# Pair 0 of an attention kernel: key loads on 64 partitions, early value loads, another order of the first loads, and identity transposes inside the first tile

## The chip, the cores and the metric

The kernel runs on one core of a Trainium2 chip. The metric is device time in microseconds (us) of one execution. Engines are named as in the profile: PE is the matrix engine (PEld its weight loads), DVE the vector engine, ACT the scalar engine, POOL is GpSimd, SP issues the loads and stores.

## What is computed

Attention, then a feed-forward block with an ELU, then a gated block with a norm ahead of it. The change touches only the start of the attention. Cut to that:

```python
B, H, S, D = 2, 8, 1152, 64
q_pool = q.reshape(B, H, S // 2, 2, D).mean(axis=3)      # 576 pooled queries a head
scores = (1 / sqrt(D)) * q_pool @ k.transpose(0, 1, 3, 2)  # 576 x 1152 a head
attn = softmax(scores)
out = attn @ v                                           # then the two blocks
```

## The kernel before

**Heads and tiles.** The 16 heads are taken as 8 pairs. A pair has 9 tiles of 128 query columns against all 1152 keys (TILES, line 30): four of each head and one, number 2 (M = 2), that holds the 64 queries left over of both heads. One loop step (line 531) makes one tile's scores (emit_S: 6 matmuls of 384 keys, 12 for tile 2), transposes the tile of two steps earlier (emit_T: 9 PE transposes, each group of three copied by ACT and DVE), runs 8 matmuls against the values (AV), and takes the exponential (emit_exp, ACT). DVE reads each score tile out of its PSUM bank (line 332); the bank has one buffer, so the scores of the next step wait for that. Pair 0 takes its tiles in the order 0, 1, 3, 4, 2, 5, 6, 7, 8, so head 1 comes first and tile 2, the first to need head 0, is step 4. Later pairs take them as numbered, so tile 2 of pair 1 is step 11.

**Two parts of each number.** Queries, keys and values are split into a rounded part and the rest (hi and lo) by two instructions, on ACT and DVE, or on POOL alone. For keys the product needs the rounded part on partitions 0 to 63 and the rest on 64 to 127. The key array in memory holds each head's 64 rows twice, so one load brings both copies to 128 partitions; hi is made on all 128 and lo then overwrites the upper 64 (prep_k).

**Loads.** All loads are issued by SP in program order, and a load whose buffer is not free holds all that stand behind it. Keys come in two halves of 576 columns (288 KB as loaded), the queries of a head in one load of 576 KB (two numbers to be added for each pooled query, line 292), the values in one of 288 KB. Raw keys and values share two buffers (tag raw), the raw queries have one (rawq); the two key halves of head 0 of pair 0 use the buffers of the later weight loads (rawk0). The queries of head 1 of pair 0 (rawq0) are loaded and prepared in three pieces.

**Order of preparation.** After pair 0's own first parts, each step prepares what jobs lists for it (line 457) and then issues the load of the next part in that list (fetch). Written as kind, pair, head, half, the list begins k 0 0 1 (step 0), v 0 1 (step 2), q 1 1 and v 0 0 (step 3), k 1 1 0 and k 1 1 1 (step 4), v 1 1 (step 5), q 1 0, k 1 0 0, k 1 0 1 (steps 6 to 8). From step 4 on POOL does all of it, in this order. After step 4's parts SP also issues the two first weight loads of 512 KB (ws.load). Ahead of the loop stand 24 identity transposes on PE (line 482), into a PSUM tile that nobody reads.

Of the kernel before, what the change touches and what calls it, by code (L numbers as in the profile page):

```python
# [20 lines left out]
QS = 576  # L21
# [18 lines left out]
def tile_kernel(ctx: ExitStack, tc: tile.TileContext, qd, kd, vd, w1d, w2d, wgd, wvd, wod, rgd, outd):  # L40
    nc = tc.nc
    V, G, T, PE, SP = nc.vector, nc.gpsimd, nc.scalar, nc.tensor, nc.sync
# [4 lines left out]
    ident = const.tile([128, 128], F32, name="ident")  # L47
# [26 lines left out]
    class Stream:  # L74
# [12 lines left out]
        def load(self, n):  # L87
            while self.loaded < min(n, len(self.srcs)):
                i = self.loaded
                t = wp.tile([128, 512, 2], U32, tag="wr", name="wr", bufs=2 if wide else 3)  # L90
                r = t.rearrange("p c w -> p (c w)")
                if wide:
                    SP.dma_start(out=r, in_=self.srcs[i].bitcast(U32))
                else:
                    t = f(r)[:, 0:512]
                    SP.dma_start(out=t, in_=self.srcs[i])
                self.raw[i] = t
                self.loaded += 1
# [171 lines left out]
    def load(kind, p, j, half=0):  # L270
        if kind == "q":
            t = ap.tile([128, 2, QS], F32, tag="rawq", name="rawq", bufs=1)
            SP.dma_start(out=t, in_=qd[2 * p + j].rearrange("p (u c) -> p u c", u=2))
        elif kind == "k":
            if (p, j) == (0, 0):
                t = f(wp.tile([128, 512, 2], U32, tag="wr", name="rawk0", bufs=2 if wide else 3).rearrange("p c w -> p (c w)"))[:, 0:QS]
            else:
                t = ap.tile([128, QS], F32, tag="raw", name="rawk", bufs=2)
            SP.dma_start(out=t, in_=kd[2 * p + j][:, half * QS:(half + 1) * QS])
        else:  # L280
            t = ap.tile([128, 9, 64], F32, tag="raw", name="rawv", bufs=2)
            SP.dma_start(out=t, in_=vd[2 * p + j].rearrange("p (k d) -> p k d", k=9))
        return t

    def prep_q(p, j, t, eng, cols=((0, QS),)):

        hi, lo = eng
        if (p, j) not in QD:
            QD[p, j] = qt[len(QD) % 3]
        d, qp = QD[p, j], t[:, 0, :]  # L290
        for a, b in cols:
            (V if hi is hi_dve else G).tensor_tensor(out=qp[:, a:b], in0=qp[:, a:b], in1=t[:, 1, a:b], op=ALU.add)
            h, l = (d[:, u, 64 + a:64 + b] for u in range(2))
            hi(h, qp[:, a:b])
            lo(l, qp[:, a:b], h)

    def prep_k(p, j, half, t, eng):
        hi, lo = eng
        if half == 0:
            KD[p, j] = ap.tile([128, S], F32R, tag="kd", name="kd", bufs=3)  # L300
        d = KD[p, j][:, half * QS:(half + 1) * QS]
        hi(d, t)
        lo(d[64:128], t[64:128], d[64:128])

    def prep_v(p, j, t, eng):
        hi, lo = eng
# [4 lines left out]
    POOL, DVE = (hi_pool, lo_pool), (hi_dve, lo_dve)  # L311
# [5 lines left out]
    def emit_S(p, i):  # L317
        if i == 0:
            st[p] = ap.tile([128, 4, NPT, 1], F32, tag="st", name="st", bufs=2)
        s = (tp if (p, i) == (0, 1) else sp).tile([128, 3, 512], F32, tag="s", name="s", bufs=1)  # L320
        if i == M:
            parts = [(QD[p, j][:, u, c:c + 128], KD[p, j]) for j, c in ((1, 0), (0, 576)) for u in (0, 1)]
        else:
            j, c, _, _, _ = TILES[i]
            parts = [(QD[p, j][:, u, c:c + 128], KD[p, j]) for u in (0, 1)]
        for n, (a, b) in enumerate(parts):
            for m in range(3):
                PE.matmul(s[:, m, 0:384], lhsT=a, rhs=b[:, 384 * m:384 * m + 384],  # L328
                          start=n == 0, stop=n == len(parts) - 1)
        pt = P[p, i] = ap.tile([128, 3, 384], F32, tag="p", name="p", bufs=3)  # L330

        V.tensor_scalar(out=pt, in0=s[:, :, 0:384], scalar1=-0.0625, scalar2=None,  # L332
                        op0=ALU.mult, op1=ALU.min, accum_out=st[p][:, 0, TILES[i][4], :])
# [106 lines left out]
    ACT = (lambda o, i: T.copy(o, i), lo_dve)  # L440

    def do_prep(u, eng):
        {"q": prep_q, "k": prep_k, "v": prep_v}[u[0]](*u[1:], raws.pop(u), eng)

    raws = {}

    def fetch(u):
        if u not in raws:
            raws[u] = load(*u)
# [7 lines left out]
    jobs = {n: [] for n in range(-1, ns)}  # L457
    for n in range(ns):
        p, k = n // NPT, n % NPT
        if p == 0:  # L460
            u = {0: [("k", 0, 0, 1)], 2: [("v", 0, 1)], 3: [("v", 0, 0)]}.get(k, [])
            jobs[n] += u
        if k in plan and not (p == 0 and k == 1):
            u = plan[k](p)
            if u[1] < 8:
                jobs[n + (p == 0 and k < 4)].append(u)
    order = [u for n in range(ns) for u in jobs[n]]
    t = ap.tile([128, 3, 384], F32, tag="p", name="rawq0", bufs=3).rearrange("p a b -> p (a b)")
    t = t.rearrange("p (u c) -> p u c", u=2)
    q01 = qd[1].rearrange("p (u c) -> p u c", u=2)  # L470
    SP.dma_start(out=t[:, :, 64:320], in_=q01[:, :, 64:320])
    fetch(("k", 0, 1, 0))
    fetch(("k", 0, 1, 1))
    for a, b in ((320, 576), (0, 64)):
        SP.dma_start(out=t[:, :, a:b], in_=q01[:, :, a:b])
    first = [("q", 0, 0), ("k", 0, 0, 0)]
    for u in first + order[:1]:
        fetch(u)

    warm = pp.tile([128, 512], F32, tag="o", name="warm", bufs=2)  # L480
    for n in range(24):
        PE.transpose(warm[:, 0:128], ident, ident)
    prep_q(0, 1, t, DVE, ((64, 320),))
    do_prep(("k", 0, 1, 0), ACT)
    do_prep(("k", 0, 1, 1), ACT)
    prep_q(0, 1, t, POOL, ((320, 576), (0, 64)))
    SP.dma_start(out=rg, in_=rgd)
    for u in first:
        do_prep(u, (ACT[0], lo_pool) if u[0] == "k" else POOL)

    def overwrites(i, g):

# [38 lines left out]
    for step in range(ns):  # L531
        emit_S(*steps[step])
        if step == 1:
            tctx.close()
            tp = actx.enter_context(tc.tile_pool(name="psT", bufs=1, space=PSUM))
            tbank = lambda: tp.tile([128, 512], F32, tag="t", name="t", bufs=3)

        due = [w for w in later if w[0] <= step]
        if step >= LT and not due:
            do_T(step)  # L540
        for w in due:
            later.remove(w)
            w[1]()
        do_AV(8, lambda p: later.append((step + 2, lambda: emit_x(p, emit_scale(p)))))
        if step >= LT and due:
            do_T(step)
        emit_exp(*steps[step])
        if step >= LT:
            if steps[step - LT][1] == NPT - 1:
                emit_r(steps[step - LT][0])  # L550
            after_T(step)
        for u in jobs.get(step, []):
            do_prep(u, (ACT[0], lo_pool) if step < 4 and u[0] != "q" else POOL)
            n = order.index(u)
            if n + 1 < len(order):
                fetch(order[n + 1])
        if step == 4:
            ws.load(2)
        ws.step(0, early_ops.get(steps[step], 0))
# [35 lines left out]
    def bank():  # L595

        nonlocal nbank
        n, nbank = nbank % 7, nbank + 1
        if n == 5 and len(psb) == 1:
            with tc.using_default_side("right"):  # L600
                psb.append(ctx.enter_context(tc.tile_pool(name="psC", bufs=2, space=PSUM)))
                ws.bank = ctx.enter_context(tc.tile_pool(name="psW", bufs=1, space=PSUM))
        return psb[n >= 5].tile([128, 512], F32, tag="b", name="b", bufs=2 if n >= 5 else 5)[:, 0:CH]
# [51 lines left out]
    for hf in range(2):  # L655
# [30 lines left out]
        if hf:  # L686
            T.activation(out=dummy, in_=eps, func=AF.Sqrt)
            for c in range(3):
                for n in range(4):
                    m, q = 2 + n // 2, n % 2  # L690
                    if q == 0:
                        b = bank()
# [86 lines left out]
    def unit(i, c, between=None):  # L779
        b = bank(), bank()  # L780
        for n in range(2):
            product(b[n], ws.get(2 * n + i + wi), xchunk(c), True, True)
            if between and n == 0:
                between()
        return i, c, *b
# [14 lines left out]
    first = [unit(0, 0)]  # L800
# [10 lines left out]
    u = [up.tile([128, 12, CH], F32, name=f"u{c}", tag=f"u{c}") for c in range(2)]  # L811
# [46 lines left out]
    b = Branch(2)  # L858
    run([(b, 1), (b, 8), (b, 9), (b, 2)], 2, 4, 2)
    run([(b, 6), (b, 5)], 2, 5)  # L860
    old, b = b, Branch(3)
    run([(b, 1), (old, 7)], 2, 5)
    for n in range(3, 11):
        if n > 3:
            old, b = b, Branch(n)
# [7 lines left out]
    b = Branch(11)  # L873
# [87 lines left out]
```

## Time and profile before

| | us |
|---|---|
| median of 3 runs | 681.26 |
| lowest and highest | 680.08, 681.34 |
| profiled execution, its own time | 681.72 |
| its span, first to last instruction | 679.9 |

| engine | busy us | share of the span |
|---|---|---|
| PE | 668.2 | 98% |
| DVE | 470.1 | 69% |
| ACT | 461.9 | 68% |
| POOL | 407.3 | 60% |

The span leaves out 1.8 us of the execution's own time. Busy time of PE is modelled from pipelined matmuls, so 98% says that PE seldom stands still, and not that it runs at its peak. The mean granted clock of PE over the span is 0.997 of full speed (2.4 GHz).

### The profile page before, as it was taken

The numbers are of one execution on the slowest core, as the hardware profiler recorded it, in microseconds if no ns is written. First come the engines' busy times: TensorE is split into PE (matmuls) and PEld (weight loads), VectorE is DVE, ScalarE is ACT, GpSimd is POOL, SyncE is SP. The second block draws the span as 40 slices with busy tenths as digits, with TensorE's granted clock in tenths as the row PEclk, the third lists the DMA queues.
The fourth block names the chain that finished last, engine by engine and source line by source line (L and its number), as shares of the span: only waits on it lengthen the run. The fifth ranks groups of instructions, "written<-read, shape, count | busy, mean of one in ns | idle before, by whom it ended". The sixth has DMA issues, their size and how long they took to land.

```text
span 679.9 us, 11376 instructions
## 1 busy us (share of the span) xinstructions
PE 668.2 (98%) x4183; PEld 658.0 (97%) x4183; DVE 470.1 (69%) x803; ACT 461.9 (68%) x921; POOL 407.3 (60%) x366
## 2 busy tenths in 40 slices
PE   7999999999999999999999999999999999999997
PEld 6999999999999999999999999999989999999997
DVE  5989998998999875765345656388777776776300
ACT  5988889898988977994458884455667644655300
POOL 5788898988989324773324443457889865313300
PEclk8999999999999999999999999999999999999999
DMA  5532234233223001224231123010334322204200
GB/s 171 206 104 88 91 126 147 88 106 119 88 88 113 25 1 53 90 90 140 94 123 63 63 94 124 31 63 32 125 98 148 124 66 93 94 1 152 73 36 36
DMA packets 21608, 62.34 MB, mean 92 GB/s; under 512 B 2736, under 2 KB 4784, under 8 KB 21552
## 3 DMA queue, kind: packets, MB, share of 16 engines
q1 hardware_dynamic: 21552, 61.62, 27.1%
q8 instruction: 33, 0.54, 0.3%
q14 instruction: 23, 0.19, 0.1%
HBM read 59.25 MB, written 2.36 MB: 91 GB/s over the span
## 4 chain that ended last, share of the span: by engine, by line
PE 87%; POOL 4%; DVE 3%; ACT 3%; DMA 2%; issue 1%; SPq 0%; POOLq 0%; DVEq 0%; ACTq 0%
PE b L216 15%; PE b L217 15%; PE b L218 15%; PE s L328 11%; PE o L372 10%; PE b L714 10%; PE t L346 10%; DMA rawk<-in_k_dram 1%; DVE x L804 1%; POOL kd L64 1%; POOL vd L64 1%; ACT xh L647 1%; ACT p L337 1%; PE t L407 1%; DMA wr<-in_wg_dram 0%
## 5 line engine op out<-in xcount | busy, mean ns | idle before, releaser
L64 POOL TENSOR_TENSOR wl<-wt,wh 128x512 fp32r<-128x512 f32 x68 | 91.6, 1348 | 96.0 <-ACT wh L183 94.7
L217 PE MATMUL b<-xl,wh 128*128 128x384 f32 x356 | 119.8, 337 | 0.0
L216 PE MATMUL b<-xh,wh 128*128 128x384 f32 x356 | 119.8, 337 | 0.0
L218 PE MATMUL b<-xh,wl 128*128 128x384 f32 x356 | 119.7, 336 | 0.0
L332 DVE TENSOR_SCALAR_CACHE_REDUCE p<-s 128x1152 f32<-128x1152 f32 x72 | 97.4, 1353 | 18.8 <-PE s L328 18.4
L70 DVE TENSOR_TENSOR ptl<-t,pth 128x384 fp32r<-128x384 f32 x216 | 106.6, 548 | 3.5 <-ACT pth L354 2.6
L354 ACT CAST pth<-t 128x384 fp32r<-128x384 f32 x216 | 89.2, 487 | 24.2 <-PE t L346 23.4
L328 PE MATMUL s<-kd,qt 128*128 128x384 f32 x480 | 99.1, 344 | 3.7 <-DVE kd L70 2.0
L337 ACT ACTIVATE p<-p,st 128x1152 f32<-128x1152 f32 x72 | 91.5, 1271 | 1.7 <-DVE p L332 1.4
L328 PEld LDWEIGHTS s<-kd,qt 128*128 128x128 f32 x480 | 83.1, 191 | 5.7 <-DVE kd L70 2.5
L346 PE MATMUL t<-ident,p 128*128 128x128 f32 x648 | 85.4, 275 | 0.4 <-DVE p L332 0.4
L372 PE MATMUL o<-pth,vd 128*128 128x256 f32 (+1 forms) x288 | 84.4, 315 | 0.0
L346 PEld LDWEIGHTS t<-ident,p 128*128 128x128 f32 x648 | 73.9, 141 | 6.7 <-DVE ptl L70 3.8
L372 PE MATMUL o<-ptl,vd 128*128 128x256 f32 (+1 forms) x288 | 78.4, 294 | 0.0
L131 DVE TENSOR_SCALAR wm<-wm 128x512 f32<-128x512 f32 x62 | 43.1, 695 | 40.1 <-ACT wm L122 39.9
L217 PEld LDWEIGHTS b<-xl,wh 128*128 128x128 f32 x356 | 66.9, 188 | 0.5 <-POOL xl L64 0.5
L216 PEld LDWEIGHTS b<-xh,wh 128*128 128x128 f32 x356 | 66.9, 188 | 0.1
L218 PEld LDWEIGHTS b<-xh,wl 128*128 128x128 f32 x356 | 66.9, 188 | 0.0
L120 ACT ACTIVATE we<-wr 128x512 uint32<-128x512 uint32 x68 | 45.4, 667 | 26.6 <-DMA wr<-in_wo_dram 13.8
L64 POOL TENSOR_TENSOR gl<-e,gh 128x384 fp32r<-128x384 f32 x37 | 38.9, 1056 | 41.0 <-ACT gh L237 41.0
L216 PE MATMUL b<-gh,wh 128*128 128x384 f32 x180 | 60.9, 338 | 0.0
L218 PE MATMUL b<-gh,wl 128*128 128x384 f32 x180 | 60.5, 336 | 0.0
(183 smaller groups left out, 1520.6 us busy)
## 6 DMA issues: line engine op xcount, KB each, us to landing
wr<-in_w_dram SPq DMA_DIRECT2D x32, 512.0 KB, 3.2
rawk<-in_k_dram SPq DMA_DIRECT2D x32, 288.0 KB, 3.0
rawq<-in_q_dram SPq DMA_DIRECT2D x15, 576.0 KB, 4.0
wr<-in_wg_dram SPq DMA_DIRECT2D x12, 512.0 KB, 3.2
wr<-in_wv_dram SPq DMA_DIRECT2D x12, 512.0 KB, 3.2
wr<-in_wo_dram SPq DMA_DIRECT2D x12, 512.0 KB, 3.3
rawv<-in_v_dram SPq DMA_DIRECT2D x16, 288.0 KB, 2.8
out_dram<-o SPq DMA_DIRECT2D x12, 192.0 KB, 1.8
```

The lines of the kernel that those rows point to most:

```text
L64: G.tensor_tensor(out=o, in0=i, in1=f(h), op=ALU.subtract)
L70: V.tensor_tensor(out=o, in0=i, in1=f(h), op=ALU.subtract)
L216: PE.matmul(out, lhsT=wh[:, k, :], rhs=ah, start=first and k == 0, stop=False)
L217: PE.matmul(out, lhsT=wh[:, k, :], rhs=al, start=False, stop=False)
L218: PE.matmul(out, lhsT=wl[:, k, :], rhs=ah, start=False, stop=last and k == 3)
L328: PE.matmul(s[:, m, 0:384], lhsT=a, rhs=b[:, 384 * m:384 * m + 384], start=n == 0, stop=n == len(parts) - 1)
L332: V.tensor_scalar(out=pt, in0=s[:, :, 0:384], scalar1=-0.0625, scalar2=None, op0=ALU.mult, op1=ALU.min, accum_out=st[p][:, 0, TILES[i][4], :])
L337: T.activation(out=pt, in_=pt, func=AF.Exp, scale=-1.0, bias=st[p][:, 0, TILES[i][4], :], accum_out=st[p][:, 1, TILES[i][4], :])
L346: PE.transpose(ps[:, k, :], src[:, 128 * b:128 * b + 128], ident)
L354: T.copy(oh, re(ps))
L372: PE.matmul(self.o[:, 0:self.N], lhsT=v[:, b, :], rhs=(pth, ptl)[u][:, g["buf"], b, g["c0"]:320], start=self.n == 0, stop=self.n == 17)
L714: PE.matmul(out, lhsT=a[x][:, k, :], rhs=b[y][:, k, :], start=first and (k, x, y) == (0, 0, 0), stop=last and (k, x, y) == (1, 1, 0), skip ...
```

## The change

Six edits, all in the start of pair 0:

- the key halves of pair 0 are loaded to 64 partitions only (144 KB instead of 288 KB); hi goes to partitions 0 to 63, and lo reads those and writes 64 to 127
- the first key half of head 0 is issued by ACT's queue (T), all others by SP as before
- the first query piece (256 columns) is cut in two of 128; the second is prepared on DVE after both key halves
- head 0's keys are loaded and prepared ahead of its queries, both halves before the loop; its queries are prepared in two pieces, the 64 columns that tile 2 needs first
- both value loads of pair 0 are issued at once at the start; in step 3, v 0 0 is prepared ahead of q 1 1 instead of behind it
- the first tile goes third by third, both halves of the sum each, with 8 identity transposes between the first third and the second

```diff
+            if p == 0:
+                t = t[0:64]
+            (T if (p, j) == (0, 0) else SP).dma_start(out=t, in_=kd[2 * p + j][0:t.shape[0], half * QS:(half + 1) * QS])
...
-        hi(d, t)
-        lo(d[64:128], t[64:128], d[64:128])
+        if p == 0:
+            hi(d[0:64], t)
+            lo(d[64:128], t, d[0:64])
+        else:
+            hi(d, t)
+            lo(d[64:128], t[64:128], d[64:128])
...
+        first = (p, i) == (0, 0)
+        for m, n in [(m, n) for m in range(3) for n in range(2)] if first else [(m, n) for n in range(len(parts)) for m in range(3)]:
+            if first and (m, n) == (1, 0):
+                warming(8)
+            a, b = parts[n]
+            PE.matmul(s[:, m, 0:384], lhsT=a, rhs=b[:, 384 * m:384 * m + 384],
+                      start=n == 0, stop=n == len(parts) - 1)
...
-            u = {0: [("k", 0, 0, 1)], 2: [("v", 0, 1)], 3: [("v", 0, 0)]}.get(k, [])
-            jobs[n] += u
+            u = {2: [("v", 0, 1)], 3: [("v", 0, 0)]}.get(k, [])
+            jobs[n] = u + jobs[n]
...
-    SP.dma_start(out=t[:, :, 64:320], in_=q01[:, :, 64:320])
+    load_q(64, 192)
     fetch(("k", 0, 1, 0))
     fetch(("k", 0, 1, 1))
-    for a, b in ((320, 576), (0, 64)):
-        SP.dma_start(out=t[:, :, a:b], in_=q01[:, :, a:b])
-    first = [("q", 0, 0), ("k", 0, 0, 0)]
-    for u in first + order[:1]:
+    load_q(192, 320)
+    load_q(320, 576)
+    load_q(0, 64)
+    for u in ("k", 0, 0, 0), ("k", 0, 0, 1), ("q", 0, 0), *order[:2]:
         fetch(u)
...
-    prep_q(0, 1, t, DVE, ((64, 320),))
+    warming(24)
+    prep_q(0, 1, t, DVE, ((64, 192),))
     do_prep(("k", 0, 1, 0), ACT)
     do_prep(("k", 0, 1, 1), ACT)
+    prep_q(0, 1, t, DVE, ((192, 320),))
     prep_q(0, 1, t, POOL, ((320, 576), (0, 64)))
     SP.dma_start(out=rg, in_=rgd)
-    for u in first:
-        do_prep(u, (ACT[0], lo_pool) if u[0] == "k" else POOL)
+    for half in range(2):
+        do_prep(("k", 0, 0, half), (ACT[0], lo_pool))
+    prep_q(0, 0, raws.pop(("q", 0, 0)), POOL, ((512, 576), (0, 512)))
```

load_q(a, b) is the SP load of columns a to b that stood there before; warming(n) is n identity transposes into the PSUM tile that the 24 already used.

## Rows read from the trace of the kernel before

**Rows 1.** Waits of PE over the whole run: us in total, times, longest

```profile
PE s L328 <- DVE kd L70: 2.0, 2, 1.7
PE b L714 <- POOL tsl L64: 1.6, 1, 1.6
...
PE s L328 <- POOL kd L64: 0.6, 1, 0.6
```

**Rows 2.** Timeline of PE: start, length (us), work, count [idle before <-releaser]

```profile
1.36 4.44 PE L482 MATMUL warm<-ident 128*128 128x128 f32 x24 [1.36 <-POOL ident masks.py:199]
6.13 0.44 PE L328 MATMUL s<-kd,qt 128*128 128x384 f32 x1 [0.33 <-DVE kd L70]
8.29 4.80 PE L328 MATMUL s<-kd,qt 128*128 128x384 f32 x17 [1.71 <-DVE kd L70]
...
18.16 2.32 PE L328 MATMUL s<-kd,qt 128*128 128x384 f32 x12 [0.82 <-DVE p L332]
...
41.16 1.41 PE L328 MATMUL s<-kd,qt 128*128 128x384 f32 x7
43.13 1.15 PE L328 MATMUL s<-kd,qt 128*128 128x384 f32 x5 [0.56 <-POOL kd L64]
```

**Rows 3.** Stretches: busy us (instructions) of PE, PEld, DVE, ACT, POOL; PE's granted clock; loads

```profile
4.75:5.80 1.05, 1.05 (x10) 0.81 (x8) 0.88 (x2) 0.54 (x1) 0.00 (x0) 1.00 1.02 291
5.80:8.20 2.40, 0.44 (x1) 0.19 (x1) 1.00 (x2) 0.67 (x1) 0.62 (x1) 0.98 0.99 364
8.20:11.50 3.30, 3.21 (x10) 3.21 (x11) 1.24 (x2) 0.67 (x1) 2.96 (x7) 0.50 0.56 210
```

**Rows 4.** Timeline of POOL, the first 43 us

```profile
7.58 1.25 POOL L292 TENSOR_TENSOR rawq<-rawq 128x256 f32<-128x256 f32 x1 [6.27 <-DMA rawq<-in_q_dram]
...
9.40 0.73 POOL L64 TENSOR_TENSOR qt<-rawq,qt 128x256 fp32r<-128x256 f32 x1
10.09 0.32 POOL L292 TENSOR_TENSOR rawq<-rawq 128x64 f32<-128x64 f32 x1
...
11.11 1.43 POOL L292 TENSOR_TENSOR rawq<-rawq 128x576 f32<-128x576 f32 x1
...
14.87 2.80 POOL L64 TENSOR_TENSOR kd<-rawk,kd 64x576 fp32r<-64x576 f32 x2
...
24.37 0.68 POOL L61 TENSOR_SCALAR kd<-rawk 128x576 fp32r<-128x576 f32 x1
...
34.95 1.43 POOL L292 TENSOR_TENSOR rawq<-rawq 128x576 f32<-128x576 f32 x1 [3.22 <-DMA rawq<-in_q_dram]
...
41.66 1.41 POOL L64 TENSOR_TENSOR kd<-rawk,kd 64x576 fp32r<-64x576 f32 x1
```

**Rows 5.** Timelines of ACT (first row) and DVE

```profile
4.62 0.67 ACT L440 CAST kd<-rawk 128x576 fp32r<-128x576 f32 x1 [2.39 <-DMA rawk<-in_k_dram]
...
7.48 0.76 DVE L70 TENSOR_TENSOR kd<-rawk,kd 64x576 fp32r<-64x576 f32 x1 [1.40 <-ACT kd L440]
10.29 1.36 DVE L332 TENSOR_SCALAR_CACHE_REDUCE p<-s 128x1152 f32<-128x1152 f32 x1 [2.06 <-PE s L328]
```

**Rows 6.** Single loads issued at 1.45, 2.07, 2.54, 14.82, 24.43: KB, us from issue to landing

```profile
rawk<-in_k_dram SPq DMA_DIRECT2D x1, 288.0 KB, 3.1
...
rawk<-in_k_dram SPq DMA_DIRECT2D x1, 288.0 KB, 4.7
...
rawq<-in_q_dram SPq DMA_DIRECT2D x1, 256.0 KB, 5.0
...
rawq<-in_q_dram SPq DMA_DIRECT2D x1, 576.0 KB, 3.7
...
rawk<-in_k_dram SPq DMA_DIRECT2D x1, 288.0 KB, 2.7
```

**Rows 7.** Timeline of SP's load issues

```profile
2.54 1.20 SPq L475 DMA_DIRECT2D rawq<-in_q_dram  x2
...
26.60 0.33 SPq L282 DMA_DIRECT2D rawv<-in_v_dram  x1
...
27.92 0.43 SPq L273 DMA_DIRECT2D rawq<-in_q_dram  x1
```

More of the change, by code (lines that the diff above doesn't have):

```diff
@@ L278, in load @@
                 t = ap.tile([128, QS], F32, tag="raw", name="rawk", bufs=2)
-            SP.dma_start(out=t, in_=kd[2 * p + j][:, half * QS:(half + 1) * QS])
+            if p == 0:
+                t = t[0:64]
+            (T if (p, j) == (0, 0) else SP).dma_start(out=t, in_=kd[2 * p + j][0:t.shape[0], half * QS:(half + 1) * QS])
         else:
@@ L325, in emit_S @@
             parts = [(QD[p, j][:, u, c:c + 128], KD[p, j]) for u in (0, 1)]
[L326 to L329, printed above, removed]
+        first = (p, i) == (0, 0)
[5 more added lines that the diff above has]
+                      start=n == 0, stop=n == len(parts) - 1)
         pt = P[p, i] = ap.tile([128, 3, 384], F32, tag="p", name="p", bufs=3)
@@ L470, in tile_kernel, with load_q, warming @@
     q01 = qd[1].rearrange("p (u c) -> p u c", u=2)
-    SP.dma_start(out=t[:, :, 64:320], in_=q01[:, :, 64:320])
+    def load_q(a, b):
+        SP.dma_start(out=t[:, :, a:b], in_=q01[:, :, a:b])
+    load_q(64, 192)
     fetch(("k", 0, 1, 0))
     fetch(("k", 0, 1, 1))
-    for a, b in ((320, 576), (0, 64)):
-        SP.dma_start(out=t[:, :, a:b], in_=q01[:, :, a:b])
-    first = [("q", 0, 0), ("k", 0, 0, 0)]
-    for u in first + order[:1]:
+    load_q(192, 320)
+    load_q(320, 576)
+    load_q(0, 64)
+    for u in ("k", 0, 0, 0), ("k", 0, 0, 1), ("q", 0, 0), *order[:2]:
         fetch(u)
     warm = pp.tile([128, 512], F32, tag="o", name="warm", bufs=2)
-    for n in range(24):
-        PE.transpose(warm[:, 0:128], ident, ident)
-    prep_q(0, 1, t, DVE, ((64, 320),))
+    def warming(n):
+        for _ in range(n):
+            PE.transpose(warm[:, 0:128], ident, ident)
+    warming(24)
+    prep_q(0, 1, t, DVE, ((64, 192),))
     do_prep(("k", 0, 1, 0), ACT)
     do_prep(("k", 0, 1, 1), ACT)
+    prep_q(0, 1, t, DVE, ((192, 320),))
     prep_q(0, 1, t, POOL, ((320, 576), (0, 64)))
     SP.dma_start(out=rg, in_=rgd)
-    for u in first:
-        do_prep(u, (ACT[0], lo_pool) if u[0] == "k" else POOL)
+    for half in range(2):
+        do_prep(("k", 0, 0, half), (ACT[0], lo_pool))
+    prep_q(0, 0, raws.pop(("q", 0, 0)), POOL, ((512, 576), (0, 512)))
     def overwrites(i, g):
```

## The prediction

> **What bounds the kernel now.** I read the waits of PE first. The change is confined to pair 0, and PE waits for little anywhere: 2.0 us in the first tile for the keys that DVE finishes, 0.6 us for keys that POOL finishes, and much later 1.6 us in another stage [rows 1]. So PE sets the time wherever it doesn't wait, and the question is what those early waits are worth. The timeline of PE places them. The 24 identity transposes end at 5.80; one matmul of the first tile runs at 6.13; then PE stands until 8.29 for the second key half. The 0.56 us for POOL stand at 43.13, inside step 11: tile 2 of pair 1 has run its seven first matmuls and waits for the last key half of head 0 of that pair [rows 2].
>
> That second wait is the important one. The timeline of POOL shows why it is there. POOL prepares everything for pair 1 in one long queue, and the last piece ends at 41.66 + 1.41 = 43.07, which releases PE at 43.13 [rows 2, 4]. Back from there POOL works without a pause to 34.95, where it had waited 3.22 us for the raw queries of pair 1's head 0 [rows 4]. That load was issued at 27.92, behind a value load issued at 26.60 and two weight loads of 512 KB [rows 7]. The value load waited for the buffer of the first key half of pair 1, which POOL began at 24.37 and so let go about 2.2 us later [rows 4, 7]. So step 11 goes on at a time that POOL's queue and SP's queue set, not PE: a fixed 16.5 us after the key half is prepared (43.07 - 26.57). **Whatever PE gains before step 11, it waits out there, unless that key half is prepared earlier too.**
>
> **The first tile.** Removed: half of the bytes of four key loads, 128 of the query columns ahead of them, and the wait for the second half with one matmul done. The first key half keeps its place in SP's queue (1.45, landing 3.1 us later [rows 6]). The second landed 4.7 us after its issue at 2.07, with 832 KB of loads up to and with it; now these are 416 KB. A single load of 288 KB took 2.7 us [rows 6], so it lands between 4.75 and 6.75; I take 5.0, near the lower end, since the bytes ahead halve. ACT's copy (0.67) and DVE's rest (0.76 [rows 5]) go by columns, not partitions, so I keep both: keys ready at about 6.45. PE is held by its transposes to 5.80, runs two matmuls at 0.18 each (12 took 2.32 us with the tail of the last [rows 2]), and 8 transposes at 0.105 (ten in 1.05 us [rows 3]) or at 0.185 (24 in 4.44 us [rows 2]): to 7.0 or 7.6. Four more matmuls end at 7.7 to 8.4. DVE reads the tile from about 7.9 instead of 10.29 [rows 5]: 2.4 us earlier. The added transposes cost 0.8 to 1.5 us of PE, of which 0.3 to 0.9 lie beside the wait for the keys. Had they cost all of it, it would still vanish in step 11.
>
> The second tile then runs at once and at full clock, where before its scores ran at half clock in part (0.50 from 8.2 to 11.5 [rows 3]); that gives 0.3 us more. Step 4, at 18.16 before [rows 2], needs head 0's keys; POOL had them at 14.87 + 2.80 = 17.67 [rows 4] and now has them near 13 (below), so POOL holds nothing there. I take PE to be 2.6 us ahead from step 4 on, between 2.0 and 3.0. It reaches step 11 at 38.6 instead of 41.16.
>
> **POOL's queue, where the end is set.** Its first work is the third query piece. That load is now fourth behind the first instead of third: two pieces were issued in 1.20 us from 2.54 [rows 7], so it moves from 2.54 to about 3.14, with less ahead of it. It landed 5.0 us after its issue [rows 6]; now between 2.7 us (5.85) and as late as before (7.58). POOL's first addition took 1.25 us where a subtraction of the same 256 columns took 0.73 [rows 4], while DVE's key subtraction ran from 7.48 to 8.24 [rows 5]: it ended 0.6 after DVE was done. The Trainium skill, GPSIMD Engine Reference, Key points, says that POOL shares its SBUF interfaces with DVE and contends with DVE instructions that have two SBUF inputs; by that rule the new DVE piece, right behind the keys, holds POOL as well, and the row agrees. DVE's keys end at 6.45, and three instructions of 128 columns follow, each a third of the 0.76 at most: about 7.3. With the same 0.6 behind it I end this addition at 7.95 (8.83 before; bounds 5.85 + 0.73 = 6.6, and 8.83).
>
> From there, in the new order: the rest of head 1's queries 11.11 - 8.83 = 2.28; two key halves 2.80; queries of head 0, 3.76 before (14.87 - 11.11), now a piece of 64 columns at 11.11 - 10.09 = 1.02 and one of 512 at 3.76 x 512/576 = 3.34 [rows 4]. Sum 9.44, so the raw query buffer is free at 17.4, where it was free at 14.87 before: POOL now does the keys first. No row shows POOL reading partitions 0 to 63 and writing 64 to 127; the bounds are no change and twice the 1.40 us of a half, and I take no change, since the same operation in place is the nearest row.
>
> The next load, queries of pair 1's head 1, waits for that buffer: issued at 17.4 instead of 14.82. It took 3.7 us with a value load beside it [rows 6]; that load now goes at the start, so I take 3.5. POOL fills the time with the two value parts (1.4 each, to 20.3), then stands until 20.9. The queries take 3.76: 24.7. The key half takes 2.2: 26.9, against 26.57. **So step 11 is released 0.3 us later**, not 2.6 earlier: the gain of 0.9 us at POOL's start is spent on the split queries (+0.6) and on a load that now starts after its buffer is late. Bounds: 6.6 for the addition gives -1.0, 8.83 with 3.7 us for the load +1.4. All else moved costs nothing: ACT issues one key load while it stands idle until 4.62 [rows 5], SP saves that issue, the value loads stand behind all that is needed early, and their copies on ACT end before POOL comes to them.
>
> **The wait and the clock.** PE's wait in step 11 grows from 0.56 to about 0.56 + 2.6 + 0.3 = 3.5 us, with one matmul in it. There is a row for such a pause: from 5.80 to 8.29 PE ran one matmul, and its granted clock then was 0.50, the 1.2 GHz level, for the 3.3 us from 8.2 to 11.5 [rows 2, 3]. At 43 us PE has no slack, so 3.3 us at half clock cost at most 1.65 us. If the clock falls before the wait ends, part of the slow stretch is spent standing; I take 0.7 us for that, and (3.3 - 0.7)/2 = 1.3 us. Lower bound 0. The Trainium skill, TensorE: Matmul & The Clock Gate, "HAM oscillation", tells of a kernel whose bursts of matmuls are parted by waits for loads and start at the throttled clock each time; by that rule the burst after step 11 starts slow.
>
> **Sum.** +0.3 (release of step 11) + 1.3 (clock) = +1.6 us. The profiled execution took 681.72 (span 679.9 and 1.8 around it), so its like would take 683.3. It stands 0.46 above the median of the runs, 681.26; against that I forecast 682.9.
>
> **Rivals.**
> - *Same wait, no fall of the clock.* The pause is cut by a matmul of step 11 and comes after a long busy stretch, where the row's pause came after a slow start. Then only the release counts, -0.3 to +0.7: 681.6. For it: the pauses of 0.82 and 0.56 us [rows 2] lowered nothing, since a mean clock of 0.997 over 679.9 us leaves 2.0 us lost, little more than the one slow stretch. Against: the row's pause was shorter than the one forecast. Chance 0.26.
> - *The gain passes: faster.* The place is the load released by pair 1's key half. If the third query piece lands by 5.9 and DVE doesn't hold POOL, the release comes 1.0 earlier; if the load issued at 27.92, which took 7.0 us to 34.92, also comes 1.0 sooner because fewer loads stand around it, step 11 goes on 2.0 earlier, the wait shrinks to 1.2 us and the clock holds: 679.3. It decides from a release 1.4 us earlier on. Against: bytes behind 26.60 are the same, and POOL's start is worth 1.0 at most. Chance 0.14.
> - *POOL is later still.* If writing to other partitions costs POOL double (+2.8), or the third piece lands no earlier (+1.4), the release is late by 1.4 to 3 us and the clock falls as well: about 684.4. Chance 0.10.
>
> **Chances and range.** The forecast has 0.50, its own range 681.7 to 683.7 (release -0.3 to +0.7, clock 0.8 to 1.65). A measurement tells 0.2%, 1.36 us, from no change. Of the forecast's half, some 0.34 lies above 682.62 and 0.16 below; with the rivals: slower 0.44, same 0.42, faster 0.14. The range leaves out most of the faster case and the worst of the late one: 680.5 to 684.2.
>
> **What would show it.** Right: first score read by DVE near 8 us; step 4 near 15.5; POOL idle for some 0.6 us before the queries of pair 1's head 1; the key half of pair 1 ended near 26.9; a PE wait of about 3.5 us that ends at 43.4 with POOL's keys as releaser; a stretch of granted clock 0.50 around 43 to 46. Wrong: that last key half done before 41.7, PE's wait in step 11 under 1.5 us, or no stretch of half clock after it.

## The result, and the profile after

The changed kernel took 684.70 us, the median of 7 runs (682.88 to 686.43); the kernel before, in 7 runs on the same chip, 681.01 (680.08 to 681.71). The ratio is 1.0056, with an interval from 1.0036 to 1.0075: slower, by 3.7 us. 682.9 was forecast, within 680.5 to 684.2. The profiled execution of after took 684.70 (span 682.9), that of before 681.72: the traces stand 3.0 us apart, and it is these 3.0 that they can explain.

One thing has to be put right first. The text ahead of the prediction says that ACT's queue issues the first key half of head 0. The condition in the code holds for both halves of that head, so ACT's queue issues two loads of 144 KB; its row stands below.

The view of PE's waits over the whole run (us in total, times, longest), which answers to [rows 1], shows the trade that was made. The wait of 2.0 us for DVE's keys is down to 0.8. The wait for POOL's keys is up from 0.6 to 2.4.

```profile
PE s L337 <- POOL kd L64: 2.4, 2, 1.8
PE s L337 <- DVE p L341: 1.8, 4, 0.7
...
PE s L337 <- DVE kd L70: 0.8, 1, 0.8
```

The timeline of PE places them, as in [rows 2].

```profile
7.56 0.61 PE L337 MATMUL s<-kd,qt 128*128 128x384 f32 x2 [0.82 <-DVE kd L70]
8.01 1.04 PE L496 MATMUL warm<-ident 128*128 128x128 f32 x8
...
17.52 2.33 PE L337 MATMUL s<-kd,qt 128*128 128x384 f32 x12 [0.68 <-DVE p L341]
...
40.56 1.23 PE L337 MATMUL s<-kd,qt 128*128 128x384 f32 x6
...
42.39 0.44 PE L337 MATMUL s<-kd,qt 128*128 128x384 f32 x1 [0.60 <-POOL kd L64]
44.63 1.97 PE L337 MATMUL s<-kd,qt 128*128 128x384 f32 x5 [1.80 <-POOL kd L64]
...
49.29 1.21 PE L337 MATMUL s<-kd,qt 128*128 128x384 f32 x6
```

Step 4 starts at 17.52 instead of 18.16, and step 11 at 40.56 instead of 41.16: the start of the kernel did become 0.6 us faster. Then step 11 stands twice for POOL's keys and goes on at 44.63, where before it went on at 43.13: 1.50 later. Step 12 starts at 49.29. The kernel before started it here:

```profile
46.33 1.21 PE L328 MATMUL s<-kd,qt 128*128 128x384 f32 x6
```

That is 2.96 us earlier, the whole distance between the two profiled executions. 1.50 of it is the release. The other 1.46 lies between the release and step 12, and the view of stretches (us, then busy us and instructions of PE, PEld, DVE, ACT and POOL, PE's granted clock, loads) shows what it is: from 44.4 on, 0.2 us before the second pause ends, the granted clock is 0.50, the 1.2 GHz level, for 3.40 us.

```profile
40.50:44.40 3.90, 1.73 (x9) 1.15 (x7) 2.08 (x4) 1.62 (x3) 3.65 (x4) 1.00 0.27 70
44.40:47.80 3.40, 3.17 (x12) 3.13 (x13) 1.16 (x1) 0.00 (x0) 3.23 (x5) 0.50 0.73 269
47.80:51.20 3.40, 3.40 (x28) 3.37 (x27) 2.36 (x6) 3.36 (x8) 1.61 (x3) 1.00 0.32 87
```

Why POOL's keys are late stands in the timeline of POOL, which answers to [rows 4].

```profile
7.84 0.98 POOL L294 TENSOR_TENSOR rawq<-rawq 128x256 f32<-128x256 f32 x1 [6.54 <-DMA rawq<-in_q_dram]
...
11.28 2.79 POOL L64 TENSOR_TENSOR kd<-rawk,kd 64x576 fp32r<-64x576 f32 x2
...
17.24 1.29 POOL L64 TENSOR_TENSOR qt<-rawq,qt 128x512 fp32r<-128x512 f32 x1
...
22.39 1.42 POOL L294 TENSOR_TENSOR rawq<-rawq 128x576 f32<-128x576 f32 x1 [0.79 <-DMA rawq<-in_q_dram]
...
26.81 1.43 POOL L64 TENSOR_TENSOR kd<-rawk,kd 64x576 fp32r<-64x576 f32 x1
...
36.48 1.44 POOL L294 TENSOR_TENSOR rawq<-rawq 128x576 f32<-128x576 f32 x1 [3.09 <-DVE p L341]
...
43.18 1.40 POOL L64 TENSOR_TENSOR kd<-rawk,kd 64x576 fp32r<-64x576 f32 x1
```

POOL starts at 7.84 (7.58 before) and lets the raw query buffer go at 18.53, where before it was free at 14.80 (the next load was issued at 14.82). The queries of pair 1's head 1 are issued then and reach POOL at 22.39, with POOL standing for 0.79. The first key half of that pair ends at 28.24 instead of 26.57, the load behind it reaches POOL at 36.48 instead of 34.95, and the last key half ends at 44.58 instead of 43.07. The view names DVE as the releaser at 36.48; DVE was long done, and I read the load issued at 29.58 as what came last; e4 bears that out. The issues of ACT's and then SP's queue:

```profile
0.90 1.40 ACTq L281 DMA_DIRECT2D rawk<-in_k_dram  x2
```

```profile
18.56 0.33 SPq L273 DMA_DIRECT2D rawq<-in_q_dram  x1
...
29.58 0.43 SPq L273 DMA_DIRECT2D rawq<-in_q_dram  x1
```

The single loads issued at 1.45, 2.09 and 3.36 answer to the first three of [rows 6]. The two key halves of head 1 have half the bytes of before. The first took 4.6 us from issue to landing instead of 3.1, the second 4.7 as before. The third query piece landed at 3.36 + 4.4 = 7.8; before it was 2.54 + 5.0 = 7.5.

```profile
rawk<-in_k_dram SPq DMA_DIRECT2D x1, 144.0 KB, 4.6
...
rawk<-in_k_dram SPq DMA_DIRECT2D x1, 144.0 KB, 4.7
...
rawq<-in_q_dram SPq DMA_DIRECT2D x1, 256.0 KB, 4.4
```

And the first tile's score is read at 10.21, all but where it was (10.29 [rows 5]), since DVE's second query piece stands ahead of it and each of its three instructions is slow beside POOL's first ones (timeline of DVE; the first line is the same addition of the first piece, with POOL idle):

```profile
3.78 0.29 DVE L294 TENSOR_TENSOR rawq<-rawq 128x128 f32<-128x128 f32 x1 [2.04 <-DMA rawq<-in_q_dram]
...
8.26 0.71 DVE L294 TENSOR_TENSOR rawq<-rawq 128x128 f32<-128x128 f32 x1
9.00 0.39 DVE L67 CAST qt<-rawq 128x128 fp32r<-128x128 f32 x1
9.43 0.85 DVE L70 TENSOR_TENSOR qt<-rawq,qt 128x128 fp32r<-128x128 f32 x1
10.21 1.34 DVE L341 TENSOR_SCALAR_CACHE_REDUCE p<-s 128x1152 f32<-128x1152 f32 x1
```

### The profile page after: what moved, and what is told of

Same layout as the page of the kernel before. It is cut to its first block, busy times and chain, and to the rows that moved or that the text cites. A ratio compares the mean times of both kernels' runs of the same rounds, so it can differ in the third digit from the quotient of the medians.

```text
span 682.9 us, 11400 instructions
## 1 busy us (share of the span) xinstructions
PE 670.1 (98%) x4191; PEld 659.6 (97%) x4191; DVE 470.5 (69%) x806; ACT 461.8 (68%) x921; POOL 407.2 (60%) x369
## 3 DMA queue, kind: packets, MB, share of 16 engines
q1 hardware_dynamic: 21408, 60.73, 26.9%
## 4 chain that ended last, share of the span: by engine, by line
PE 89%; DVE 4%; POOL 2%; ACT 2%; issue 1%; DMA 0%; DVEq 0%; POOLq 0%; ACTq 0%; SPq 0%
PE b L216 15%; PE b L218 15%; PE b L217 15%; PE s L337 12%; PE o L381 11%; PE t L355 10%; PE b L732 10%; DVE x L822 1%; ACT xh L665 1%; PE t L416 1%; DMA wr<-in_wg_dram 0%; POOL kd L64 0%; DVE wm L133 0%; DVE p L341 0%; ACT p L346 0%
```

## The experiments

The theory: POOL's order frees the raw query buffer late, that chain releases step 11 late, and the clock falls in the wait. The rivals tried against it: ACT's queue, the narrow key loads or the partitions they go to, and the divided first query piece. The 8 transposes in the first tile and the early value loads were not tried by themselves. Every kernel computes all of the reference; e7 adds transposes that nobody reads. Ratios are to the kernel before, run on the same chip as the experiment; since chips differ between experiments, two kernels are compared by their ratios.

### e1_sp_queue: after, with head 0's keys in SP's queue

```diff
-            (T if (p, j) == (0, 0) else SP).dma_start(
+            SP.dma_start(
```

> The changed kernel, but head 0's two key halves are issued by SP in their place and not by ACT. Theory queue: with two queues the 16 load engines share out early bandwidth, and head 1's first key half waited for head 0's; then its landing after the issue at 1.45 falls from 4.6 to about 3.2 us, the 256-column query piece lands before 7.3 instead of 7.84, the release of step 11 comes 0.3 to 0.6 us earlier than 44.6, and the time falls by about as much. Theory narrow: loads to 64 partitions are slow by themselves, whatever queue issues them; then the landing stays above 4 us and the time stays within 0.3 us, or grows by the 1.2 us of SP's issues.

Measured: 683.81 us (681.93 to 685.17, 6 runs), ratio 1.0044 [1.0028, 1.0059]. The key half of head 1 landed 3.6 us after its issue instead of 4.6, the third query piece 3.3 instead of 4.4; POOL began 1.1 earlier and step 11 was released 0.7 earlier.

```profile
6.74 1.02 POOL L294 TENSOR_TENSOR rawq<-rawq 128x256 f32<-128x256 f32 x1 [5.43 <-DMA rawq<-in_q_dram]
```

```profile
43.94 1.52 PE L337 MATMUL s<-kd,qt 128*128 128x384 f32 x5 [1.80 <-POOL kd L64]
```

What follows: the second queue delays the first by about 1 us, and by the ratios this is 0.8 of the 3.7 us. The intervals of this kernel and of after overlap; the landing times carry the reading.

### e2_wide: after, with key loads on all 128 partitions

```diff
-            if p == 0:
-                t = t[0:64]
...
-        if p == 0:
-            hi(d[0:64], t)
-            lo(d[64:128], t, d[0:64])
...
+        hi(d, t)
+        lo(d[64:128], t[64:128], d[64:128])
```

> The changed kernel, but all key loads go to 128 partitions as before (288 KB each), still with ACT's queue for head 0. Theory narrow: a packet of 2304 bytes takes as long as in the kernel before (93 ns instead of 120 to 176), twice the bytes take no longer, and head 1's keys land within 0.3 us of where the changed kernel has them; time the same within 0.5 us. Theory queue: bytes count, competition is the same or worse, and the first key half lands 0.7 us later still, the release 0.5 to 1 us later, time up by as much.

Measured: 684.50 us (683.22 to 684.81, 5 runs), ratio 1.0053 [1.0040, 1.0066], which is that of after. With twice the bytes the first key half of head 1 (288 KB) took 4.5 us to land, against 4.6 for 144 KB in after, and step 11 was released at 44.34. So at this place, halving the bytes of a key load gave nothing.

### e3_old_order: after, with POOL's first work in the order of before

```diff
-            jobs[n] = u + jobs[n]
+            jobs[n] += u
...
-    for u in ("k", 0, 0, 0), ("k", 0, 0, 1), ("q", 0, 0), *order[:2]:
+    for u in ("k", 0, 0, 0), ("k", 0, 0, 1), ("q", 0, 0), ("v", 0, 1), ("v", 0, 0):
...
+    do_prep(("q", 0, 0), POOL)
     for half in range(2):
         do_prep(("k", 0, 0, half), (ACT[0], lo_pool))
-    prep_q(0, 0, raws.pop(("q", 0, 0)), POOL, ((512, 576), (0, 512)))
```

> The changed kernel with POOL's old order: head 0's queries in one piece ahead of its keys, the queries of pair 1's head 1 ahead of the value part. Theory order: the release of step 11 is late because the raw query buffer comes free at 18.5 instead of 14.8; with the old order it is free near 14.9, the release comes back to about 43.1 from 44.6, step 4 is later by 0.3 at most, and the time falls by 1.5 us or more, to 681 to 683, the rest being clock lost in the wait. Rival: the release is late because POOL's first piece lands late; then the time stays within 0.5 us of the changed kernel.

Measured: 681.78 us (680.58 to 682.88, 11 runs), ratio 1.0016 [1.0008, 1.0025]. The queries of pair 1's head 1 were issued at 15.12 instead of 18.56, the key half ended at 27.25, and step 11 was released 0.8 earlier, after one short wait. In this profile PE reached it late (41.89), because the first tile had waited 2.4 us for DVE's keys.

```profile
41.89 1.41 PE L337 MATMUL s<-kd,qt 128*128 128x384 f32 x7
43.84 1.14 PE L337 MATMUL s<-kd,qt 128*128 128x384 f32 x5 [0.54 <-POOL kd L64]
```

What follows: by the ratios, the old order takes 2.7 of the 3.7 us away. The theory stands, for the larger part: the release came about half of the way back to the 43.13 of before. POOL's first addition still ended late, at 9.10 (8.83 before), and the key half at 27.25 (26.57 before).

### e11_order_alone: the kernel before, with the new order alone

Wide key loads, all by SP, the first query piece whole and no transposes inside the tile, as before. Only the order is new.

```diff
-            u = {0: [("k", 0, 0, 1)], 2: [("v", 0, 1)], 3: [("v", 0, 0)]}.get(k, [])
-            jobs[n] += u
+            u = {2: [("v", 0, 1)], 3: [("v", 0, 0)]}.get(k, [])
+            jobs[n] = u + jobs[n]
...
-    for u in first + order[:1]:
+    for u in ("q", 0, 0), ("k", 0, 0, 0), ("k", 0, 0, 1), *order[:2]:
...
-    for u in first:
-        do_prep(u, (ACT[0], lo_pool) if u[0] == "k" else POOL)
+    for half in range(2):
+        do_prep(("k", 0, 0, half), (ACT[0], lo_pool))
+    prep_q(0, 0, raws.pop(("q", 0, 0)), POOL, ((512, 576), (0, 512)))
```

> The kernel before with the order edits alone: head 0's keys ahead of its queries on POOL, the queries in two pieces, both value loads at once, the value part ahead of the queries of pair 1's head 1. Theory order: the raw query buffer comes free near 18.3 instead of 14.8, the key half of pair 1 ends near 28.0 instead of 26.6, step 11 is released near 44.5 instead of 43.1, PE's wait grows to about 2 us, and the time grows by 1.3 to 2.8 us, to 682.3 to 683.8. Rival: the earlier step 4 and the value loads out of the way make up for it; then the time is within 0.7 us of the kernel before.

Measured: 684.64 us (682.82 to 685.25, 6 runs), ratio 1.0052 [1.0040, 1.0064]. The profiled execution was this kernel's fastest.

```profile
17.75 1.27 POOL L64 TENSOR_TENSOR qt<-rawq,qt 128x512 fp32r<-128x512 f32 x1
...
22.79 1.43 POOL L292 TENSOR_TENSOR rawq<-rawq 128x576 f32<-128x576 f32 x1 [0.31 <-DMA rawq<-in_q_dram]
...
27.23 1.43 POOL L64 TENSOR_TENSOR kd<-rawk,kd 64x576 fp32r<-64x576 f32 x1
```

```profile
42.02 1.41 PE L328 MATMUL s<-kd,qt 128*128 128x384 f32 x7
44.15 1.15 PE L328 MATMUL s<-kd,qt 128*128 128x384 f32 x5 [0.71 <-POOL kd L64]
```

What follows: the order by itself, with no other part of the change, makes as slow a kernel as the whole change. POOL frees the buffer at 19.0 and step 11 is released at 44.15, 1.0 after that of before. The median lies above what the theory asked for, and no trace shows why. In the profile PE was late at step 11 for a wait on ACT's exponential, so this one trace does not show the full price. That wait is a second effect of the edit: ACT's copies of head 0's keys now stand ahead of the first exponential, ACT stood 4.14 us for their loads, PE 2.06 us for the exponential, and the granted clock was 0.51 from 14.1 to 17.4. In after, where these keys come early by ACT's queue, the first exponential doesn't wait for them.

### e4_weights_late: after, with the weight loads one step later

The load that releases step 11 stands in SP's queue behind two weight loads of 512 KB [rows 7]. Here these go behind it; one operation planned for that stretch moves a step later with them.

```diff
-            if step == 4:
+            if step == 5:
                 ws.load(2)
...
-    early_ops = {(0, 7): 1, (1, 1): 1,
+    early_ops = {(1, 1): 2,
```

> The changed kernel with the two first weight loads (1 MB) issued one step later, behind the queries of pair 1's head 0, and their first operation moved from step 7 to step 10. Theory: step 11 waits for POOL, POOL for these queries, and these for the 1 MB ahead of them in SP's queue; so the queries land 2 to 3 us earlier (near 33.7 instead of 36.4), step 11 is released near 42 instead of 44.6, PE's wait there falls from 2.4 to under 0.8 us, no half clock follows, and the time falls by 3 to 4 us, to 680.5 to 681.5. Rival: the wait only moves, to the later key loads behind the weights; then the time falls by less than 1 us.

Measured: 680.80 us (680.30 to 681.69, 11 runs), ratio 1.0003 [0.9995, 1.0012]: the whole loss is gone, with POOL's new order still in place. The queries (issued at 29.41, now ahead of the weights) reach POOL at 34.12 instead of 36.48, the last key half ends before PE asks for it, and step 11 runs its 12 matmuls without a pause and without a stretch of half clock.

```profile
34.12 1.44 POOL L294 TENSOR_TENSOR rawq<-rawq 128x576 f32<-128x576 f32 x1
...
40.83 1.44 POOL L64 TENSOR_TENSOR kd<-rawk,kd 64x576 fp32r<-64x576 f32 x1
```

```profile
40.92 2.55 PE L337 MATMUL s<-kd,qt 128*128 128x384 f32 x12
...
45.52 1.21 PE L337 MATMUL s<-kd,qt 128*128 128x384 f32 x6
```

What follows: the loss passes through the one wait in step 11, all of it that the times can tell. Step 12 comes 3.77 us earlier than in after; by the ratios the time falls by 3.6.

### e5_before_weights_late: the same edit in the kernel before

> The kernel before, with only the two first weight loads issued one step later, behind the queries of pair 1's head 0, and their first operation moved from step 7 to step 10. Theory: in the kernel before, step 11 waits 0.56 us for POOL and nothing else of pair 0 or 1 costs time; so the time falls by 0.3 to 0.6 us and no more. Rival: the weight loads also hold later parts; then more than 1 us is gained.

Measured: 680.47 us (679.97 to 681.76, 11 runs), ratio 0.9997 [0.9988, 1.0005]. Step 11 ran unbroken here too, from 40.27. The median is 0.5 us below that of its runs of before (680.99), as the theory asked, but the interval takes in no change. More than 1 us, the rival, is out.

### e7_fill_wait: after, with 18 transposes ahead of step 11's matmuls

```diff
+        if (p, i) == (1, M):
+            for _ in range(18):
+                PE.transpose(s[:, 0, 384:512], ident, ident)
```

> The changed kernel with 18 identity transposes ahead of the matmuls of step 11, into columns of the score banks that nobody reads. They take 2 us of the time in which PE stands there. Theory clock: the release stays near 44.6, but PE is not idle long enough for its clock to fall, no 0.50 stretch follows, the time of step 12 comes back from 49.3 to 47.8, and the time falls by about 1.4 us, to 683.3 in the median, with runs less far apart. Rival: the half clock costs nothing, because DVE, ACT or POOL hold the steps after it; then the time stays the same or grows.

Measured: 683.78 us (683.54 to 686.07, 5 runs), ratio 1.0049 [1.0037, 1.0061].

```profile
40.86 2.13 PE L335 MATMUL s<-ident 128*128 128x128 f32 x18
42.75 1.48 PE L340 MATMUL s<-kd,qt 128*128 128x384 f32 x7
44.81 1.14 PE L340 MATMUL s<-kd,qt 128*128 128x384 f32 x5 [0.58 <-POOL kd L64]
...
48.01 1.21 PE L340 MATMUL s<-kd,qt 128*128 128x384 f32 x6
```

The stretch behind the release, which ran at 0.50 in after:

```profile
44.80:48.20 3.40, 3.39 (x26) 3.38 (x27) 2.21 (x4) 1.56 (x4) 3.23 (x4) 1.00 0.67 236
```

What follows: the release is no earlier (44.81), yet the granted clock stays at full speed, the 2.4 GHz level, and step 12 comes 1.28 us earlier than in after, though released 0.18 later: 1.46 us from release to step 12. That is what the fall of the clock costs in the profiled execution of after. The rival that the wait alone makes the whole loss is out for it. The times say less: the gain is 0.9 us by the medians and 0.5 by the ratios, the intervals overlap, the runs still spread over 2.5 us, and the profile is that of one of the two fastest. The mean granted clock was 1.000 in these two (683.54 both) and 0.997 in the other three, so in those it fell somewhere.

### e8_upper: after, with head 0's narrow keys on partitions 64 to 127

```diff
-            if p == 0:
-                t = t[0:64]
+            r = slice(0, 128) if p else slice(64, 128) if j == 0 else slice(0, 64)
+            t = t[r]
...
+            hi(d[64:128], t)
+            lo(d[0:64], t, d[64:128])
```

> The changed kernel with head 0's keys loaded to partitions 64 to 127 (hi there, lo below), head 1's to 0 to 63 as before, so that the two queues write different halves at the same time. Theory destination: narrow loads are slow because 16 load engines write into half of the partitions; with both halves in use the packets of 2304 bytes go back to about 93 ns, head 1's first key half lands 3.5 us or less after its issue instead of 4.6, the third query piece lands before 7.3, and the time falls by 0.5 to 1 us. Rival (queue or source): landings stay within 0.3 us of the changed kernel, and so does the time.

Measured: 685.22 us (684.73 to 687.98, 6 runs), ratio 1.0073 [1.0060, 1.0085]; step 11 was released at 45.18. Head 1's first key half landed in 4.0 us instead of 4.6, but POOL began at 7.92, no earlier than in after. In this profile the later load of pair 1's queries took 4.6 us instead of 3.7, and POOL stood longer for it:

```profile
23.19 1.44 POOL L294 TENSOR_TENSOR rawq<-rawq 128x576 f32<-128x576 f32 x1 [1.98 <-DMA rawq<-in_q_dram]
```

What follows: that the two queues lose because they go to the same 64 partitions isn't borne out by the time; the landing moved about half of the way that the theory asked for (3.5), in one profile. Where the narrow loads lose is left open.

### e6_three: after with e1, e3 and e4 together

> The changed kernel with the three edits of the runs before together: head 0's keys issued by SP, POOL's old order, weight loads behind the queries. Theory: the faster start is worth as much as step 11 lets through. PE reaches step 11 near 39.5, POOL's last key half is done near 39.5 to 40.5 so that PE waits under 1 us, and the time falls by 1.5 to 2.5 us against the kernel before, to 678.2 to 679.2. Rival: the wait moves on to step 4 (head 0's keys behind its queries on POOL) or to tile 2 of pair 2; then the time is within 0.7 us of the kernel before.

Measured: 679.21 us (678.91 to 680.21, 11 runs), ratio 0.9976 [0.9968, 0.9985]. It beats both kernels, the one before by 0.24%.

```profile
39.62 2.27 PE L337 MATMUL s<-kd,qt 128*128 128x384 f32 x12
...
43.94 1.21 PE L337 MATMUL s<-kd,qt 128*128 128x384 f32 x6
```

Step 4 starts at 16.61 and step 11 at 39.62, unbroken. POOL's last key half ended at 39.23, just ahead of it. The 1.6 us that the start gains now reach the end: step 12 comes at 43.94, 2.4 us before that of the kernel before. Not all of the gain is the start: e5, run beside it with the late weight loads alone, lies between the two (medians 680.99 before, 680.47 e5, 679.21 here).

### e9_one_piece: e6 with the first query piece undivided

```diff
-    load_q(64, 192)
+    load_q(64, 320)
...
-    prep_q(0, 1, t, DVE, ((64, 192),))
+    prep_q(0, 1, t, DVE, ((64, 320),))
...
-    prep_q(0, 1, t, DVE, ((192, 320),))
```

> The kernel with the three edits (head 0's keys by SP, POOL's old order, weight loads behind the queries), and with the first query piece of 256 columns loaded and prepared at once on DVE again, not in two of 128. Theory port: the second piece on DVE takes 1.95 us instead of 0.8 because POOL's first three instructions run beside it, and the first score tile is read only behind it (9.30); without it that read starts near 8.7, step 11 is reached near 39.0, and the time falls by 0.4 to 0.6 us. Rival: the larger first load makes the keys land later by as much; then the time stays within 0.2 us.

Measured: 679.28 us (678.93 to 679.52, 9 runs), ratio 0.9975 [0.9966, 0.9984], the time of e6. DVE's instructions on the whole piece (0.43 us for 256 columns) now end before POOL starts, and the first score is read at 9.12 instead of 9.30, right behind PE. There the 8 transposes stand in the way: the keys were ready at 7.32, and the tile's last four matmuls began at 8.14, behind them.

```profile
4.31 0.43 DVE L294 TENSOR_TENSOR rawq<-rawq 128x256 f32<-128x256 f32 x1 [2.57 <-DMA rawq<-in_q_dram]
...
6.57 0.75 DVE L70 TENSOR_TENSOR kd<-rawk,kd 64x576 fp32r<-64x576 f32 x1 [0.18 <-ACT kd L449]
9.12 1.36 DVE L341 TENSOR_SCALAR_CACHE_REDUCE p<-s 128x1152 f32<-128x1152 f32 x1 [1.80 <-PE s L337]
```

What follows: dividing the piece is worth nothing that shows in the time, either way, as long as the transposes stand there; e6 without them was not run.

### e10_three_wide: e6 with key loads on all 128 partitions

> The kernel with the three edits, and pair 0's keys loaded to 128 partitions again. Theory narrow: half the bytes bring nothing, since a packet of 2304 bytes takes 136 ns on the mean instead of about 100; first key half ready within 0.3 us of the narrow version, time the same within 0.4 us. Rival: the bytes count, the third query piece lands 0.5 to 1 us later, time up by 0.3 to 1 us.

Measured: 680.68 us (680.34 to 682.29, 11 runs), ratio 0.9999 [0.9991, 1.0008], 1.5 us slower than e6. Here I expected wrong. The first keys were no later (DVE began them at 5.54, in e6 at 5.73), but the loads behind them were: ACT got the two key halves of head 0 at 9.14 and 10.51, in e6 at 8.18 and 9.36, and POOL the queries of head 0 at 11.96 where e6 had them at 10.68. PE felt the key halves. ACT copies them ahead of the first exponential, which so began at 11.09 although DVE had read the score by 9.92; PE stood 1.05 us for it, and behind that its granted clock was 0.51 from 13.2 to 16.2 (timelines of ACT and PE):

```profile
10.51 0.68 ACT L443 CAST kd<-rawk 128x576 fp32r<-128x576 f32 x1 [0.70 <-DMA rawk<-in_k_dram]
11.09 1.25 ACT L340 ACTIVATE p<-p,st 128x1152 f32<-128x1152 f32 x1
```

```profile
12.49 1.98 PE L349 MATMUL t<-ident,p 128*128 128x128 f32 x9 [1.05 <-ACT p L340]
```

Step 4 came at 17.89 and step 11 at 40.90, 1.28 after that of e6. What follows: half the bytes do pay, for the loads that stand behind head 1's keys and not for those keys themselves. The fall of the clock is not all of the difference: the five runs with a mean granted clock of 1.000 took 680.34 to 680.77, still 1.1 us or more above e6's median.

## Why the prediction was right or wrong

Right were the direction and the mechanism: the gain of the first tile is waited out in step 11, POOL's late query buffer sets when that step goes on, and the clock falls in the wait. e4 shows the first (the wait away, the loss away), e3 and e11 the second, and the stretch of 0.50 in after, gone in e7, the third. Wrong was a size, and it is the step "**So step 11 is released 0.3 us later**": measured, it was 1.50 later.

| step | forecast | measured |
|---|---|---|
| first score read by DVE | 7.9 | 10.21 |
| step 4 starts | 15.5 | 17.52 |
| step 11 reached | 38.6 | 40.56 |
| POOL's first addition ends | 7.95 | 8.82 |
| from there to the free query buffer | 9.44 | 9.71 |
| issue of the next load until POOL starts on it | 3.5 | 3.83 |
| POOL idle before it | 0.6 | 0.79 |
| key half of pair 1 ends | 26.9 | 28.24 |
| step 11 released, against before | +0.3 | +1.50 |
| PE's wait in step 11 | 3.5 | 2.40 |
| cost of the half clock | 1.3 | 1.46 |

**What was mis-sized.** The release term was summed from three pieces, and all three came out longer. POOL's first addition ended 0.87 later than taken, the rest of the queue took 0.27 more, the load 0.33 more; together 1.47, less 0.1 in the instructions between that load and the end of the key half. From the key half to the last one it then took 16.34 where 16.5 was counted on, so the release was 1.2 later than forecast. The first is the largest, and its reason is in the loads: half the bytes were taken to land sooner. The second key half was put at 5.0 and landed at 6.8, as before; the third query piece landed at 7.8, 0.2 later than the late end of its bounds. Some 1 us of these landings is ACT's queue beside SP's; the rest is that narrow loads at this place land no sooner than wide ones (e2). For the addition ACT's queue is enough: without it (e1) it ended at 7.76, ahead of the 7.95 forecast. The prediction said that ACT's issue costs nothing because ACT stands idle. It asked what the issue costs ACT and not what that queue's bytes cost SP's loads, and it counted one load there where there are two.

**The bounds.** The late end of the release was given as +1.4, with 8.83 for the addition. The forecast's own range then took only +0.7 of it. 8.82 was measured, at that late end. The mis-sized pieces close the profiled execution: 683.3 was summed for it, 1.2 more release and 0.16 more clock give 684.66, and it took 684.70. The remaining 0.46 of the miss is the step from the profiled execution to the median: before's profile stood that much above the median that the forecast was set against, and after's happens to stand on its own.

**The first tile.** Its gain was put at 2.4 us and was 0.1, since the keys of the second half came no earlier (DVE ended them at 8.23, before at 8.24 [rows 5]) and the second query piece stood ahead of the first score: 1.95 us for three instructions, where the first piece took 0.81. The prediction cost them at 0.76 at most and let them lie beside PE. The GPSIMD Engine Reference of the Trainium skill, Key points, which the prediction drew on for POOL, names the contention with DVE's two-input instructions and not which engine pays. Here these, of 0.71 and 0.85 us, paid more than POOL's addition (0.98, against 0.73 for the subtraction in [rows 4]). What gain there was by step 4, 0.64, came for the most part from the second tile at full clock, as forecast, only larger than the 0.3 given: DVE read its score 0.48 earlier (11.49, before 11.97). The rest is ACT, which no longer copies a key half between its first two exponentials (0.66 us from 12.95 before). None of this reached the end: PE's smaller gain made a shorter wait (2.40 instead of 3.5) and left the release as it was. e9 says the same of the divided piece, in a kernel where such a gain could pass, though the transposes let only 0.18 us of it through there (9.30 to 9.12).

**The clock.** 1.3 was forecast and 1.46 measured. The first rival, the same wait and no fall of the clock, is out for the profiled execution: the clock fell in the second of two pauses of 0.60 and 1.80 us with one matmul between them. The "HAM oscillation" section of TensorE: Matmul & The Clock Gate in the Trainium skill agrees: the burst behind a wait started slow, and with the wait filled (e7) it did not. The rival isn't out for every run: in the two fastest of the seven, 682.88 and 683.06, the mean granted clock was 1.000, and in the other five 0.996 to 0.998. Those two lost about 2 us without it.

**The other rivals.** "The gain passes" needed a release 1.4 us earlier, and it came 1.50 later. "POOL is later still", 684.4, came nearest to the time, for one of its two reasons: the third query piece landed no earlier. The other, a price for writing to other partitions, was nothing (2.79 us for two, 2.80 before). It was given 0.10.

**What stays open.** Runs of after spread over 3.5 us, those of kernels without the wait in step 11 over 0.6 to 2.0 (e9 the least, e10 the most). Why some runs of after reach 686 is not settled; the clock does not order them, since the three slowest have 0.998 and the run of 683.74 has 0.996. e8 shows that the load of pair 1's queries can take 0.9 us longer and that POOL then stands for it, in one profile of another kernel.

## What to carry to other kernels

Before you credit a faster start, find the next place where an in-order queue has a deadline, and work out that queue's time from the edit: here POOL's order kept a single raw buffer 3.7 us longer, and 26 us after that it set the end. When a load is late, look at what stands ahead of it in its queue: putting two weight loads behind it undid the loss (e4), and with the order put back and one queue for the early loads the faster start paid at last (e6, 0.9976). A cost with bounds far apart should carry both ends into the range.

## What the runs showed of the hardware that was not expected

- **Half the bytes on half the partitions landed no sooner.** 144 KB to 64 partitions took 4.6 us, 288 KB to 128 partitions 4.5, both with two queues at work (after, e2); with one queue 3.5 and 3.4 (e6, e10). The bytes still counted for the loads behind: the queries of head 0 took 4.6 us in e6 and 6.3 in e10.
- **A second queue delays the first.** With ACT's two loads of 144 KB moved into SP's queue, the first key half landed in 3.6 us instead of 4.6 and a query piece in 3.3 instead of 4.4 (e1).
- **DVE and POOL slow each other, and the one that began second paid.** The same addition of 128 columns took DVE 0.29 us with POOL idle and 0.71 begun 0.42 us into POOL's first addition (after). In e8 DVE began it 0.03 us ahead of POOL's and took 0.29 again; its copy behind, begun beside POOL's addition, took 0.64 instead of 0.23. POOL paid in before: its addition, begun 0.10 us behind DVE's subtraction, took 1.25, and 0.73 in e10, where it began first.
- **The clock's fall cost as much as the later release.** Two pauses of 2.40 us in all brought 3.40 us at half clock, 1.46 us lost beside 1.50 for the release; with 18 transposes of 2.13 us in the wait the clock stayed up in the profiled execution (e7).
